# A block's forward and backward pass: issuing every TensorE product and transpose as four 32-column matmuls

## The chip, the cores and the metric

The kernel runs on one core of a Trainium2 chip. The time is the device time in microseconds (us) from the first to the last instruction of one execution. In the text PE is TensorE (PEld its weight loads), DVE is VectorE, ACT is ScalarE, POOL is GpSimd and SP is SyncE, as the profile names them.

## The reference

One transformer block with 2048 tokens of 512 features, in bfloat16: layer norm, local attention with 32 heads of 16 features over 8 earlier positions at a distance of 2, a residual, a second layer norm, a feed-forward part of width 1792 with GELU, and a second residual. The kernel returns the block's output and the gradients of the input and of six parameters.

```python
def _A_ref(x, wqkv, wo):                 # S=2048, H=32 heads, Dh=16, W=8, dil=2
    q, k, v = split_heads(x @ wqkv)
    idx = pos[:, None] - arange(W) * dil # -1e9 where idx < 0
    logits = einsum("bhsd,bhswd->bhsw", q, k[idx]) * Dh ** -0.5
    o = einsum("bhsw,bhswd->bhsd", softmax(logits), v[idx])
    return merge_heads(o) @ wo
def _B_ref(x, w1, b1, w2, b2):
    return gelu(x @ w1 + b1) @ w2 + b2
h = x + _A_ref(layernorm(x), A_wqkv, A_wo)
h2 = h + _B_ref(layernorm(h), B_w1, B_b1, B_w2, B_b2)
# outputs: h2 and the vjp of grad_out for A_x, A_wqkv, A_wo, B_w1, B_b1, B_w2, B_b2
```

## The kernel before

The 2048 tokens are worked on in four chunks of 512 (`CH`), a chunk as four tiles of 128 tokens. The code describes about 1970 operations (`op(...)`: an engine, an estimated time, a function that emits the instructions, and the buffers it reads and writes). The table `ORDER` at the end of the file is the order in which they are emitted, over all stages and engines at once, and `HOMES` gives each buffer its place in SBUF or its PSUM bank. `Plan.emit` goes through `ORDER`; each engine gets its own instructions in that order, and waits between engines follow from the buffers.

The stages overlap. Roughly, in the order of time:

- The first 156 us: per chunk the layer norm, the projections to q, k and v (`p1_proj`, L626, and `p1_v`), the transposes that bring tiles from token-major to feature-major form and back (`to_fm_tiles`, L416; `to_tm_store`, L434), the attention scores (`p1_attn`: VectorE multiplies, L479, and TensorE adds up with a 0/1 matrix, L487), the softmax sums (L702), the weighted sum of v (`p1_o`, whose `band` multiplies on VectorE, L518, and adds up on TensorE, L527), its transposes (`turn`, L543), the output projection and the second layer norm.
- 156 to about 325 us: the feed-forward part and its backward pass (`p2_h`, `p2_out`, `p2_bwd`), which are 512-column products on TensorE and elementwise work on VectorE and ScalarE.
- After that: the backward pass of the attention (`p3_go`, `p3_dots`, with row sums at L919; `p3_bands`, three more rounds of `band` and `turn` for the gradients of q, v and k; `p3_gl1`), and between its steps the weight gradients (`wg_group`), which depend on little and fill TensorE. The products of the last weight gradient (evicted to `wgsq`) end the program.

Names in the rows: `ps` is any PSUM bank; `prf`, `prb`, `prbo`, `prbq`, `prbv` and `prbk` are VectorE's products; `S` the 0/1 matrices; `kt`, `qt`, `ln`, `ost`, `gqs`, `gks`, `gvs` tiles that are transposed; `e` and `pp` the operands of the 128-column sums (L702 and L919); `gw1in`, `gw2in`, `xw1in`, `xw2in`, `ro`, `gq3in` reloaded operands of the weight gradients; `got` the gradient of the attention's output; `wz` a zeroed tile for fillers at the start, which are run while the first loads come in (`warm`, L311 and L316).

TensorE's matmul takes a stationary operand (a weight load, `LDWEIGHTS`) of up to 128 columns, each of which becomes an output partition, and streams the other operand, up to 512 columns, past it. Two forms stand in the kernel. In the full form, one load of 128 columns and one matmul write 128 partitions. In the quarter form, four loads of 32 columns and four matmuls, each into its own 32 partitions, do the same product; the profile shows them as `128*32`. Three kinds of work have the quarter form by need, since each quarter has its own operand or output (`cls=1`): the projections at L626 and the sums at L487 and L527. For the products that go through `mmul` with 512 columns (`cls=4`) `Plan.emit` chooses: a run of them between two operations of `cls=1` gets the quarter form (`quad`, L268), any other run the full form (L270). Products with 256 columns, transposes, the sums at L702 and L919 and the fillers always have the full form. In this order the two forms meet at 34 places of TensorE.

```python
                if o.cls == 4:
                    run.append(i)
                else:
                    if prev == 1 and o.cls == 1:
                        quad.update(run)
                    run, prev = [], o.cls
```

Of the kernel before, what the change touches and what calls it, by code (L numbers as in the profile page):

```python
# [10 lines left out]
P = 128  # L11
# [7 lines left out]
W = 8  # L19
# [42 lines left out]
class Plan:  # L62
# [7 lines left out]
    def sb(self, name, shape, dt=BF16):  # L70
        n = int(np.prod(shape[1:])) * (4 if dt == F32 else 2)
        b = Buf(name, "sb", shape, dt, (n + 63) // 64 * 64)
        self.bufs.append(b)
        return b
# [43 lines left out]
    def emit(self, order, homes):  # L118

        nc = self.nc  # L120
        assert sorted(order) == list(range(len(self.ops))) and len(homes) == len(self.bufs)
        at = {i: n for n, i in enumerate(order)}
        assert all(at[p] < at[o.i] for o in self.ops for p in o.preds)
        last = {}
        for i in order:
            for b in self.ops[i].bufs:
                if b.space != "fix":
                    last[id(b)] = at[i]
        ps = nc.alloc_psum_tensor("ps", [P, NBANK * BANK], F32).ap()
        for b, h in zip(self.bufs, homes):  # L130
            b.home = h if b.space == "ps" else self.base + h * 64
            assert b.home + b.need <= (NBANK if b.space == "ps" else self.top)
        quad, run, prev = set(), [], 0
        for i in order:
            o = self.ops[i]
            if o.eng == "PE":
                if o.cls == 4:
                    run.append(i)
                else:
                    if prev == 1 and o.cls == 1:  # L140
                        quad.update(run)
                    run, prev = [], o.cls
        live = []
        for n, i in enumerate(order):
            o = self.ops[i]
            for b in o.bufs:
                if b._ap is None and b.space != "fix":
                    live = [x for x in live if last[id(x)] >= n]
                    assert all(x.space != b.space or x.home + x.need <= b.home or b.home + b.need <= x.home for x in live), (b.name, o.tag)
                    live.append(b)  # L150
                    if b.space == "ps":
                        b._ap = ps[:, b.home * BANK:(b.home + b.need) * BANK]
                    else:
                        b._ap = nc.alloc_sbuf_tensor_at(f"{b.name}_{n}_{len(live)}", list(b.shape), b.dt, offset=b.home).ap()
            self.quad = i in quad
            o.fn()


# [1 line left out]
def kernel(  # L160
# [21 lines left out]
    V, A, T, G, SY = nc.vector, nc.scalar, nc.tensor, nc.gpsimd, nc.sync  # L182
# [20 lines left out]
    def cst(name, shape, dt=BF16):  # L203
        return nc.alloc_sbuf_tensor(name, list(shape), dt).ap()

    ident, Pmat, nident = (cst(n, [P, P]) for n in ("ident", "Pmat", "nident"))
# [36 lines left out]
    pl = Plan(nc, base, top)  # L243
# [19 lines left out]

    def mmul(out, l, r, start, stop):

        if pl.quad:
            for a in range(4):
                T.matmul(out[32 * a:32 * a + 32, :], lhsT=l[:, 32 * a:32 * a + 32], rhs=r, start=start, stop=stop, skip_group_check=True)  # L268
        else:
            T.matmul(out, lhsT=l, rhs=r, start=start, stop=stop, skip_group_check=True)  # L270

    def act_us(n, ptr=0, accum=False):
        return 0.055 + 0.833e-3 * n + 0.093 * ptr + (0.10 if accum else 0.0)
# [29 lines left out]
    def warm(n, more=0, each=2):  # L303

        z = sb("wz", [P, 512])
        pz = ps_("pwz")
        op("DVE", 0.2, lambda: V.memset(z(), 0.0), w=[z], tag="wz")

        def mm():
            for _ in range(n):  # L310
                T.matmul(pz(), lhsT=z()[:, 0:P], rhs=z(), start=True, stop=True)  # L311
        op("PE", 0.2157 * n, mm, r=[z], w=[pz], tag="warm")

        def mm2():
            for _ in range(each):
                T.matmul(pz(), lhsT=z()[:, 0:P], rhs=z(), start=True, stop=True)  # L316
        for _ in range(more):
            op("PE", 0.2157 * each, mm2, r=[z], w=[pz], tag="fill")

# [76 lines left out]
    def to_fm(src, dst, tag, soft=()):  # L396
        for hh in range(2):
            pt = ps_("pt" + tag)

            def tr(hh=hh, pt=pt):  # L400
                for d2 in range(2):
                    dc = 2 * hh + d2
                    for j in range(TPC):
                        T.transpose(pt.bf()[:, d2 * 512 + j * P:d2 * 512 + (j + 1) * P], src()[:, j, dc * P:(dc + 1) * P], ident[:])
            op("PE", 8 * XP, tr, r=[src, IDENT], w=[pt], tag="xp" + tag, soft=soft, lat=0.17)
            evict(dst, lambda hh=hh: dst()[:, 2 * hh:2 * hh + 2, :], pt, lambda pt=pt: pt.bf().rearrange("p (a n) -> p a n", a=2), 1024,
                  key=hh, tag="fm" + tag)

    def to_fm_tiles(src, dst, tag):

        for j in range(TPC):
            pt = ps_("pt" + tag)

            def tr(pt=pt, j=j):
                for dc in range(DC):
                    T.transpose(pt.bf()[:, dc * P:(dc + 1) * P], src()[:, j, dc * P:(dc + 1) * P], ident[:])  # L416
            op("PE", DC * XP, tr, r=[(src, j), IDENT], w=[pt], tag="xp" + tag, lat=0.17)
            evict(dst, lambda j=j: dst()[:, :, j * P:(j + 1) * P], pt, lambda pt=pt: pt.bf()[:, 0:512].rearrange("p (a n) -> p a n", a=DC), 512,
                  key=j, tag="fm" + tag)
# [5 lines left out]
    def to_tm_store(fm, off, dst, c, back, tag, pm):  # L425
        for j2 in range(TPC // 2):
            pt = ps_("ptm" + tag)

            def tr(j2=j2, pt=pt):
                for jj in range(2):  # L430
                    j = 2 * j2 + jj
                    for g in range(4):
                        o = _sub(pt.bf(), [[32, DH], [1, 8]], jj * 512 + 8 * g) if pm else pt.bf()[:, jj * 512 + g * P:jj * 512 + (g + 1) * P]
                        T.transpose(o, fm()[:, g, off + j * P:off + (j + 1) * P], (Pmat if pm else ident)[:])  # L434
            st = sb("tm" + tag, [P, 2, 512])
            op("PE", 8 * XP, tr, r=[(fm, 0), (fm, 1), PMAT if pm else IDENT], w=[pt], tag="xptm" + tag)
            evict(st, lambda st=st: st(), pt, lambda pt=pt: pt.bf().rearrange("p (a n) -> p a n", a=2), 1024, tag="tm" + tag)
            tm_store(st, dst, c, j2, back, tag)
# [97 lines left out]
    def turn(src, dst, mp, tag):  # L536

        pt = ps_("ptu" + tag)

        def tr():  # L540
            for mm in range(2):
                for k in range(4):
                    T.transpose(pt.bf()[:, mm * 512 + k * P:mm * 512 + (k + 1) * P], src()[:, 2 * mp + mm, k * P:(k + 1) * P], ident[:])  # L543
        op("PE", 8 * XP, tr, r=[(src, 2 * mp), (src, 2 * mp + 1), IDENT], w=[pt], tag="xpu" + tag)
        evict(dst, lambda: dst()[:, 2 * mp:2 * mp + 2, :], pt, lambda: pt.bf().rearrange("p (a n) -> p a n", a=2), 1024, key=mp, tag="un" + tag)

# [134 lines left out]
    def p1_attn(c):  # L681
# [4 lines left out]
        if c == 0:  # L686
            op("DVE", 0.25, lambda: V.tensor_tensor(out=L3()[0:32, :, 0:16], in0=L3()[0:32, :, 0:16], in1=mk[:], op=ALU.add), r=[MKB], w=[L], tag="mask")
        mx, e, r = sb("mx", [P, P]), sb("e", [P, W, P]), sb("r", [P, P])
        d["e"] = e
        op("DVE", 1.13, lambda: V.tensor_reduce(out=mx(), in_=L().rearrange("p (w n) -> p n w", w=W), axis=mybir.AxisListType.X, op=ALU.max),  # L690
           r=[L], w=[mx], tag="max")
# [6 lines left out]
        pss = ps_("pss", 1)  # L698

        def esum():  # L700
            for w in range(W):
                T.matmul(pss()[:, 0:P], lhsT=ident[:], rhs=e()[:, w, :], start=(w == 0), stop=(w == W - 1))  # L702
        op("PE", W * XP, esum, r=[e, IDENT], w=[pss], tag="sume")

        def recip():
# [4 lines left out]
           r=[e, r], w=[(attn, c)], tag="attn", lock=1)  # L710
# [188 lines left out]
    def p3_dots(c):  # L899
# [10 lines left out]
        pp = sb("pp", [P, W, P])  # L910
# [4 lines left out]
        pr_, sr = ps_("psr", 1), sb("sr", [P, P])  # L915

        def rowsum():
            for w in range(W):
                T.matmul(pr_()[:, 0:P], lhsT=nident[:], rhs=pp()[:, w, :], start=(w == 0), stop=(w == W - 1))  # L919
        op("PE", W * XP, rowsum, r=[pp, NID], w=[pr_], tag="rowsum")  # L920
        evict(sr, lambda: sr(), pr_, lambda: pr_()[:, 0:P], P, tag="rowsum")

        def sub():
# [4 lines left out]
           r=[L, (attn, c)], w=[(glf, c)], tag="glf")  # L928
# [169 lines left out]
    def wturn(dst, dap, src, sap, kb, key, tag):  # L1098

        pt = ps_("ptw" + tag)  # L1100

        def tr():
            for k in range(8):
                T.transpose(pt.bf()[:, k * P:(k + 1) * P], sap(k), ident[:])
        op("PE", 8 * XP, tr, r=[src, IDENT], w=[pt], tag="xp" + tag)
        evict(dst, dap, pt, lambda: pt.bf().rearrange("p (a n) -> p a n", a=kb), 1024, key=key, tag="ev" + tag)

# [4 lines left out]
    for i in range(0 if W2PE else 4):  # L1112
        r = F // 4
# [12 lines left out]
    for c in range(NC):  # L1126
        pl.stage = 9 + c
        if c == 1:
            xload(woR, lambda: woR(), lambda: A_wo, 512, tag="woT", soft=[(h_[3], 0)])
            op("ACT", act_us(4 * D), lambda: A.copy(out=woT().rearrange("p a (d h) -> p a d h", h=H), in_=_sub(woR()[:, 0, 0:1], [[D, DC], [1, DH], [DH, H]])),  # L1130
               r=[woR], w=[woT], tag="hinwo")
# [204 lines left out]
```

## Time and profile before

| | |
|---|---|
| median of three runs | 551.95 us (551.7 to 554.23) |
| span of the profiled execution | 551.9 us |
| TensorE busy | 538.8 us, 98%, 7764 matmuls |
| VectorE busy | 494.2 us, 90% |
| ScalarE busy | 324.2 us, 59% |
| mean granted TensorE clock | 0.997 |
| DMA moved | 126.68 MB, 230 GB/s |

The profile shows one execution; the only time of its own that it has is the span, from the first to the last instruction. Matmuls are pipelined: the profile shows each quarter or full matmul of 512 columns with 379 ns, though one begins every 216 ns where they follow each other. So the length of a chain piece, which goes from start to start, gives the price of a unit, and the mean duration doesn't.

### The profile page before, as it was taken

The page shows a single profiled execution, that of the slowest core. Times are in us where ns is not written, and L with a number is a line of the kernel's source. Part 1 is how long each engine was busy: PE and PEld are TensorE (multiplying, and loading weights), DVE is VectorE, ACT ScalarE, POOL GpSimd, SP SyncE. Part 2 cuts the span into 40 slices and gives each one's busy share as a digit, 9 for nine tenths or more (in the row PEclk, how much of TensorE's full clock was granted, in tenths as well). Part 3 has the DMA queues.
Part 4 walks back from the last instruction along what each step waited for, and adds up shares of the span by engine and source line. Part 5 has one row for each costly group of instructions (what it writes and reads, how often), then busy time and mean ns, then how long its engine had stood idle before and what let it go on. Part 6 is the DMA issues. An engine that isn't in the chain of part 4 may idle for free.

```text
span 551.9 us, 17462 instructions
## 1 busy us (share of the span) xinstructions
PE 538.8 (98%) x7764; PEld 286.7 (52%) x7764; DVE 494.2 (90%) x648; ACT 324.2 (59%) x507; POOL 25.8 (5%) x40
## 2 busy tenths in 40 slices
PE   7999999999989999999999999999999999999996
PEld 4756554444535445555555555465455555555542
DVE  7999999999979999999787089958899999999993
ACT  4987799989899876885341242034033376443521
POOL 1300100030001000000000000000010001000000
PEclk9999999999989999999999999999999999999999
DMA  8899998991597558679999999999999997888427
GB/s 279 226 291 281 417 302 190 201 332 83 74 235 251 137 98 197 201 121 214 197 191 219 182 194 192 291 218 281 213 279 425 335 338 284 355 290 187 128 60 190
DMA packets 195147, 126.68 MB, mean 230 GB/s; under 512 B 149760, under 2 KB 190656, under 8 KB 193024
## 3 DMA queue, kind: packets, MB, share of 16 engines
q1 hardware_dynamic: 189472, 81.79, 66.3%
q0 software_dynamic: 3408, 41.68, 19.8%
q10 hardware_dynamic: 2192, 2.10, 1.1%
q8 instruction: 60, 0.98, 0.8%
q14 instruction: 15, 0.12, 0.1%
HBM read 55.74 MB, written 35.21 MB: 165 GB/s over the span
## 4 chain that ended last, share of the span: by engine, by line
PE 55%; DVE 16%; ACT 4%; DMA 3%; issue 3%; SPq 2%; POOL 0%; ACTq 0%; DVEq 0%
PE ps L268 32%; PE ps L270 16%; PE ps L527 4%; DMA oT<-ost 2%; DVE xb L856 2%; DVE prbk L518 1%; DVE prbo L518 1%; DVE xb L803 1%; PE ps L487 1%; DVE prbv L518 1%; PE ps L543 1%; DVE x L799 1%; DVE st L360 1%; DVE h L747 1%; DVE h2s L828 1%
## 5 line engine op out<-in xcount | busy, mean ns | idle before, releaser
L479 DVE TENSOR_TENSOR prb<-got,vw 128x4096 bf16<-128x4096 bf16 x16 | 36.0, 2282 | 20.7 <-ACT got L297 13.8
L268 PE MATMUL ps<-w1T,xb 128*32 128x512 bf16 x896 | 53.1, 379 | 0.6 <-DVE h2s L828 0.4
L268 PE MATMUL ps<-goT,w2T 128*32 128x512 bf16 x832 | 50.5, 379 | 0.2 <-ACT xb L774 0.2
L297 ACT CAST wgs<-ps 128x512 bf16<-128x512 f32 (+1 forms) x30 | 16.2, 562 | 53.8 <-PE ps L270 30.4
L268 PE MATMUL ps<-w,gl 128*32 128x512 bf16 x776 | 46.3, 379 | 0.0
L856 DVE SCALAR_TENSOR_TENSOR xb<-xb,ps 128x512 bf16<-128x512 bf16 x56 | 36.9, 681 | 6.6 <-PE ps L268 6.4
L774 ACT ACTIVATE xb<-ps,b1c 128x512 bf16<-128x512 f32 x56 | 35.6, 703 | 10.1 <-PE ps L268 5.0
L268 PEld LDWEIGHTS <-xb 128*32 128x32 bf16 x896 | 26.2, 97 | 23.1 <-issue 1.2
L518 DVE TENSOR_TENSOR prbv<-Rv,cfv 128x4096 bf16<-128x4096 bf16 x16 | 35.7, 2284 | 1.4 <-PE ps L527 1.4
L518 DVE TENSOR_TENSOR prbq<-Rq,cfq 128x4096 bf16<-128x4096 bf16 x16 | 35.9, 2287 | 0.9 <-PE ps L270 0.4
L518 DVE TENSOR_TENSOR prbk<-Rk,cfk 128x4096 bf16<-128x4096 bf16 x16 | 35.9, 2284 | 0.3 <-PE ps L527 0.2
L518 DVE TENSOR_TENSOR prbo<-Ro,cfo 128x4096 bf16<-128x4096 bf16 x16 | 35.9, 2283 | 0.2
L479 DVE TENSOR_TENSOR prf<-qt,kt 128x4096 bf16<-128x4096 bf16 x16 | 35.7, 2283 | 0.0
L268 PEld LDWEIGHTS <-w2T 128*32 128x32 bf16 x832 | 24.0, 97 | 21.3 <-issue 0.5
L268 PEld LDWEIGHTS <-gl 128*32 128x32 bf16 x776 | 21.3, 97 | 21.1 <-ACT gl L777 1.3
L268 PE MATMUL ps<-wqkvT,gqkvT 128*32 128x512 bf16 x512 | 31.0, 379 | 0.0
L796 ACT ACTIVATE xb<-xb 128x2048 bf16<-128x2048 bf16 (+1 forms) x16 | 26.6, 1691 | 6.4 <-DVE xb L795 6.4
L626 PE MATMUL ps<-ln1T,wqk 128*32 128x512 bf16 x512 | 29.3, 381 | 0.7 <-ACT ln1T L297 0.7
L270 PE MATMUL ps<-ln2T,w 128*128 128x512 bf16 x120 | 27.4, 379 | 0.0
L792 ACT ACTIVATE x<-xb 128x2048 bf16<-128x2048 bf16 (+1 forms) x16 | 26.4, 1691 | 1.4 <-DVE h L747 1.3
L777 ACT ACTIVATE gl<-xb 128x2048 bf16<-128x2048 bf16 (+1 forms) x16 | 26.5, 1686 | 0.1
L561 ACT ACTIVATE gyr<-ps,rstd 128x512 bf16<-128x512 f32 x16 | 10.8, 677 | 23.5 <-PE ps L268 23.5
(199 smaller groups left out, 1085.7 us busy)
## 6 DMA issues: line engine op xcount, KB each, us to landing
Ro<-v_d POOLq DMA_DIRECT2D x4, 2304.0 KB, 11.6
Rq<-k_d POOLq DMA_DIRECT2D x4, 2304.0 KB, 11.5
Rv<-go_d POOLq DMA_DIRECT2D x4, 2304.0 KB, 13.9
Rk<-q_d POOLq DMA_DIRECT2D x4, 2304.0 KB, 14.1
g_d<-gl SPq DMA_DIRECT2D x9, 512.0 KB, 5.2
gh_d<-xb SPq DMA_DIRECT2D x9, 512.0 KB, 4.7
w<-in_B_w_dram SPq DMA_DIRECT2D x2, 1792.0 KB, 7.4
out_dram<-wgs SPq DMA_DIRECT2D x13, 256.0 KB, 4.7
```

The lines of the kernel that those rows point to most:

```text
L268: T.matmul(out[32 * a:32 * a + 32, :], lhsT=l[:, 32 * a:32 * a + 32], rhs=r, start=start, stop=stop, skip_group_check=True)
L270: T.matmul(out, lhsT=l, rhs=r, start=start, stop=stop, skip_group_check=True)
L297: fn = lambda: A.copy(out=ap(), in_=pap())
L479: op("DVE", tt_us(4096), lambda g=g, pr=pr: V.tensor_tensor(out=pr(), in0=ql()[:, g, :].unsqueeze(1).to_broadcast([P, W, 512]), in1=_sub(k ...
L518: V.tensor_tensor(out=pr().rearrange("p a j (d h) -> p a j d h", h=H), in0=_sub(R()[:, o0, 0:1], [[st, 2], [512, 4], [32, DH], [1, H]]), i ...
L527: T.matmul(ps()[32 * j:32 * j + 32, :], lhsT=S4[:], rhs=pr()[:, hf, j, :], start=(hf == 0), stop=(hf == 1), skip_group_check=True)
L626: T.matmul(ps()[32 * a:32 * a + 32, gg * 512:(gg + 1) * 512], lhsT=_sub(wq_()[:, dc, 0:1], [[DH, H]], sel * D + 4 * g + a), rhs=rhs, start ...
L774: op("ACT", act_us(512, 1), lambda f=f, ps=ps, xb=xb, f0=f0: A.activation(out=xb()[:, f - f0, :], in_=ps(), func=ACT.Identity, bias=b1c[:, ...
L777: op("ACT", act_us(N), lambda xb=xb, gl=gl: A.activation(out=fl(gl), in_=fl(xb), func=ACT.Gelu_apprx_tanh), r=[xb], w=[gl], tag="gelu", mo ...
L792: op("ACT", act_us(N), lambda xb=xb, x2=x2: A.activation(out=fl(x2), in_=fl(xb), func=ACT.Square), r=[xb], w=[x2], tag="x2")
L796: op("ACT", act_us(N), lambda xb=xb: A.activation(out=fl(xb), in_=fl(xb), func=ACT.Tanh, scale=GC), w=[xb], tag="tanh", mode=6)
L856: op("DVE", 0.61, lambda f=f, ps=ps, z=z, f0=f0: V.scalar_tensor_tensor(out=z()[:, f - f0, :], in0=z()[:, f - f0, :], scalar=1.0, in1=ps() ...
```

## The change

Every product that goes through `mmul`, the fillers, the sums at L702 and L919 and all transposes of 128 x 128 blocks (the new `turn128`) are issued in the quarter form. The choice in `Plan.emit` goes. `ORDER` and `HOMES` stay as they were, and no operation of another engine changes. The sums over eight blocks of 128 columns, formerly plain matmuls, go through `mmul` now. Two small transposes (of `b1b`, 14 rows, and `gbb`, 18 columns) keep their form. TensorE's matmuls after the change are 9224 of 512 columns, 256 of 256 and 1600 of 128, all in the quarter form, and the two small ones; before they were 6656 quarter ones of 512 columns, and 642 full ones of 512, 64 of 256 and 400 of 128.

```diff
-        quad, run, prev = set(), [], 0
-        for i in order:
...
-            self.quad = i in quad
             o.fn()
...
     def mmul(out, l, r, start, stop):
 
-        if pl.quad:
-            for a in range(4):
-                T.matmul(out[32 * a:32 * a + 32, :], lhsT=l[:, 32 * a:32 * a + 32], rhs=r, start=start, stop=stop, skip_group_check=True)
-        else:
-            T.matmul(out, lhsT=l, rhs=r, start=start, stop=stop, skip_group_check=True)
+        for a in range(4):
+            T.matmul(out[32 * a:32 * a + 32, :], lhsT=l[:, 32 * a:32 * a + 32], rhs=r, start=start, stop=stop, skip_group_check=True)
+
+    def turn128(out, src):
+
+        for a in range(4):
+            T.transpose(out[32 * a:32 * a + 32, :], src[:, 32 * a:32 * a + 32], ident[:])
...
-                T.matmul(pz(), lhsT=z()[:, 0:P], rhs=z(), start=True, stop=True)
+                mmul(pz(), z()[:, 0:P], z(), start=True, stop=True)
...
-                T.transpose(pt.bf()[:, dc * P:(dc + 1) * P], src()[:, j, dc * P:(dc + 1) * P], ident[:])
+                turn128(pt.bf()[:, dc * P:(dc + 1) * P], src()[:, j, dc * P:(dc + 1) * P])
...
-                    T.transpose(pt.bf()[:, mm * 512 + k * P:mm * 512 + (k + 1) * P], src()[:, 2 * mp + mm, k * P:(k + 1) * P], ident[:])
+                    turn128(pt.bf()[:, mm * 512 + k * P:mm * 512 + (k + 1) * P], src()[:, 2 * mp + mm, k * P:(k + 1) * P])
...
-                T.matmul(pss()[:, 0:P], lhsT=ident[:], rhs=e()[:, w, :], start=(w == 0), stop=(w == W - 1))
+                mmul(pss()[:, 0:P], ident[:], e()[:, w, :], start=(w == 0), stop=(w == W - 1))
...
-                T.matmul(pr_()[:, 0:P], lhsT=nident[:], rhs=pp()[:, w, :], start=(w == 0), stop=(w == W - 1))
+                mmul(pr_()[:, 0:P], nident[:], pp()[:, w, :], start=(w == 0), stop=(w == W - 1))
```

TensorE's instructions in the backward bands, at 446 us of the profiled execution, where the last sums of a band of v (`prbv`) are followed by eight transposes of the gradient of k (`gks`). Numbers behind a name only tell buffers apart. Before:

```order
L527 LDWEIGHTS S
L527 MATMUL ps<-prbv_36_7832,S 32x512
L543 LDWEIGHTS gks_38_7869
L543 MATMUL ps<-ident,gks_38_7869 128x128
L543 LDWEIGHTS gks_38_7869
L543 MATMUL ps<-ident,gks_38_7869 128x128
```

And the same place after the change, where line 261 is in `turn128`:

```order
L521 LDWEIGHTS S
L521 MATMUL ps<-prbv_36_10454,S 32x512
L261 LDWEIGHTS gks_38_10491
L261 MATMUL ps<-ident,gks_38_10491 32x128
L261 LDWEIGHTS gks_38_10491
L261 MATMUL ps<-ident,gks_38_10491 32x128
L261 LDWEIGHTS gks_38_10491
L261 MATMUL ps<-ident,gks_38_10491 32x128
L261 LDWEIGHTS gks_38_10491
L261 MATMUL ps<-ident,gks_38_10491 32x128
```

Nothing has moved: the two full transposes of the first piece are eight quarter ones now, the first four of which stand in the second piece, and the change of form between the sums and the transposes is gone.

TensorE's instructions in the first chunk's projections, where the last transposes of the normed input (`ln`, L416) are followed by the projection to k (`wqk`), before and then after:

```order
L416 LDWEIGHTS ln_0_23_7_136
L416 MATMUL ps<-ident,ln_0_23_7_136 128x128
L626 LDWEIGHTS wqk_6_134
L626 MATMUL ps<-ln1T_36_11_159,wqk_6_134 32x512
L626 LDWEIGHTS wqk_6_134
```

```order
L261 MATMUL ps<-ident,ln_0_23_7_166 32x128
L261 LDWEIGHTS ln_0_23_7_166
L261 MATMUL ps<-ident,ln_0_23_7_166 32x128
L620 LDWEIGHTS wqk_6_164
L620 MATMUL ps<-ln1T_36_11_213,wqk_6_164 32x512
```

The projection itself is as it was; what stands ahead of it has four times as many instructions.

More of the change, by code (lines that the diff above doesn't have):

```diff
@@ L132, in emit @@
             assert b.home + b.need <= (NBANK if b.space == "ps" else self.top)
-        quad, run, prev = set(), [], 0
-        for i in order:
[L135 to L138, printed above, removed]
-                else:
-                    if prev == 1 and o.cls == 1:
-                        quad.update(run)
-                    run, prev = [], o.cls
         live = []
@@ L264, in mmul @@
     def mmul(out, l, r, start, stop):
-        if pl.quad:
-            for a in range(4):
-                T.matmul(out[32 * a:32 * a + 32, :], lhsT=l[:, 32 * a:32 * a + 32], rhs=r, start=start, stop=stop, skip_group_check=True)
-        else:
-            T.matmul(out, lhsT=l, rhs=r, start=start, stop=stop, skip_group_check=True)
+        for a in range(4):
[3 more added lines that the diff above has]
+            T.transpose(out[32 * a:32 * a + 32, :], src[:, 32 * a:32 * a + 32], ident[:])
     def act_us(n, ptr=0, accum=False):
@@ L315, in mm2 @@
             for _ in range(each):
-                T.matmul(pz(), lhsT=z()[:, 0:P], rhs=z(), start=True, stop=True)
+                mmul(pz(), z()[:, 0:P], z(), start=True, stop=True)
         for _ in range(more):
@@ L403, in tr @@
                     for j in range(TPC):
-                        T.transpose(pt.bf()[:, d2 * 512 + j * P:d2 * 512 + (j + 1) * P], src()[:, j, dc * P:(dc + 1) * P], ident[:])
+                        turn128(pt.bf()[:, d2 * 512 + j * P:d2 * 512 + (j + 1) * P], src()[:, j, dc * P:(dc + 1) * P])
             op("PE", 8 * XP, tr, r=[src, IDENT], w=[pt], tag="xp" + tag, soft=soft, lat=0.17)
@@ L433, in tr @@
                         o = _sub(pt.bf(), [[32, DH], [1, 8]], jj * 512 + 8 * g) if pm else pt.bf()[:, jj * 512 + g * P:jj * 512 + (g + 1) * P]
-                        T.transpose(o, fm()[:, g, off + j * P:off + (j + 1) * P], (Pmat if pm else ident)[:])
+                        if pm:
+                            T.transpose(o, fm()[:, g, off + j * P:off + (j + 1) * P], Pmat[:])
+                        else:
+                            turn128(o, fm()[:, g, off + j * P:off + (j + 1) * P])
             st = sb("tm" + tag, [P, 2, 512])
@@ L1103, in tr @@
             for k in range(8):
-                T.transpose(pt.bf()[:, k * P:(k + 1) * P], sap(k), ident[:])
+                turn128(pt.bf()[:, k * P:(k + 1) * P], sap(k))
         op("PE", 8 * XP, tr, r=[src, IDENT], w=[pt], tag="xp" + tag)
```

## The prediction

> **What bounds the kernel now.** I read the page's busy times and its chain first, then the busy times by stage, then the idle times of VectorE (DVE) and the chain piece by piece in the second half. In the fence below, the first row is busy time, share of the span and instructions of each engine, the second the chain's shares, the rest busy time by stage (window, PE, PEld, DVE, ACT, POOL, granted clock, DMA share, GB/s).
>
> ```profile
> PE 538.8 (98%) x7764; PEld 286.7 (52%) x7764; DVE 494.2 (90%) x648; ACT 324.2 (59%) x507; POOL 25.8 (5%) x40
> PE 55%; DVE 16%; ACT 4%; DMA 3%; issue 3%; SPq 2%; POOL 0%; ACTq 0%; DVEq 0%
> ...
> 0.00:156.00 156.00, 148.38 (x1763) 82.75 (x1767) 150.18 (x189) 133.81 (x181) 15.23 (x22) 1.00 0.85 241
> 156.00:283.00 127.00, 126.41 (x2296) 65.31 (x2297) 117.69 (x235) 91.56 (x115) 1.48 (x1) 0.99 0.83 184
> 283.00:394.00 111.00, 110.76 (x1578) 59.85 (x1578) 80.39 (x95) 30.49 (x71) 1.13 (x2) 1.00 1.10 220
> 394.00:500.00 106.00, 105.95 (x1598) 55.17 (x1594) 103.51 (x64) 49.76 (x95) 6.88 (x13) 1.00 0.93 322
> 500.00:541.00 41.00, 41.00 (x520) 20.92 (x520) 40.06 (x64) 15.86 (x42) 0.00 (x0) 1.00 0.51 119
> ```
>
> TensorE (PE) is busy almost everywhere, at full clock, so it looks like the only bound. But VectorE is as full in two stages: 150.2 of the first 156 us, 103.5 of the 106 us from 394 to 500. There both set the time, and a shorter TensorE only waits for VectorE. TensorE alone binds from 283 to 394 us (VectorE 80.4 of 111) and after 500 us, where its last products need little of VectorE.
>
> VectorE's idle pieces after 394 us, with what ended them in brackets:
>
> ```profile
> 394.26 1.13 DVE L497 STREAM_TRANSPOSE cfq<-glf 128x512 bf16<-128x512 bf16 x1 [2.25 <-DMA tmgod<-got]
> ...
> 420.99 6.70 DVE L518 TENSOR_TENSOR prbq<-Rq,cfq 128x4096 bf16<-128x4096 bf16 x3 [0.36 <-PE ps L270]
> 435.36 2.29 DVE L518 TENSOR_TENSOR prbv<-Rv,cfv 128x4096 bf16<-128x4096 bf16 x1 [1.08 <-PE ps L527]
> ...
> 506.24 2.29 DVE L518 TENSOR_TENSOR prbv<-Rv,cfv 128x4096 bf16<-128x4096 bf16 x1 [0.28 <-PE ps L527]
> ```
>
> From 436 to 506 us VectorE never waits for TensorE: a gain of TensorE there can't move it.
>
> **What a unit of TensorE costs.** Call one former 128-column matmul, or four 32-column ones that take its place, a unit. The chain (start, us, what) gives its price in both forms, and that of a change of form:
>
> ```profile
> 283.25 38.60 PE ps L268 x712
> ...
> 339.12 1.83 PE ps L270 x8
> ...
> 417.86 0.45 PE ps L543 x8
> 418.30 3.45 PE ps L270 x16
> ...
> 426.55 0.55 PE ps L527 x8
> ...
> 431.43 3.45 PE ps L268 x64
> ...
> 523.91 17.39 PE ps L270 x80
> ```
>
> Sixteen full products of 512 columns take 3.45 us, 216 ns each; 64 quarter ones take 3.45 us too, 216 ns for four. So in the 512-column products (624 of L270 in 18 groups, of which the first and the last stand here, and 18 fillers) the two forms cost the same: 0 for these, with a long sustained case behind it (712 in 38.60 us, 54 ns per quarter). Eight full transposes take 0.45 us, 56 ns each.
>
> ```profile
> L270 PE MATMUL ps<-ln2T,w 128*128 128x512 bf16 x120 | 27.4, 379 | 0.0
> ...
> L270 PE MATMUL ps<-gqs,ln1b 128*128 128x512 bf16 x4 | 1.0, 382 | 0.0
> ```
>
> A change of form shows as a surcharge: 1.83 instead of 1.73 us for eight full products after quarter ones, 0.55 instead of 0.43 for eight quarter ones after transposes. It is 0.10 to 0.12 us, and the chain shows it where the neighbours follow without a wait.
>
> **The change, part by part.**
>
> (1) Changes of form that go. TensorE's order has 34 places where a full unit and a quarter unit meet: 19 before 156 us, four between 339 and 381 us, ten between 409 and 476 us, one at 523.91 us. At about 0.1 us each that is 3.4 us of TensorE's time. What reaches the end:
> - The 19 before 156 us: VectorE is at 150.2 of 156 us there; TensorE's gain turns into idle time before VectorE's next product. I take 0.
> - The four at 339 to 381 us: 0.4 us of TensorE, while VectorE waits for it. But VectorE's next stop, at 394.26 us, is a transfer of got (2.25 us), which was made earlier. Between 0 and 0.4; I take 0.1, since that transfer is what ends the wait.
> - The ten at 409 to 476 us: 1.0 us of TensorE. Two of them lie before the wait of 1.08 us at 435.36 us and shorten it by 0.2; the other eight fall where VectorE doesn't wait. I take 0.2.
> - The one at 523.91 us: 0.12 (17.39 against 80 x 0.216 = 17.28), all of it at the end, since only wgq products and their eviction follow.
> - The wait at 506.24 us, 0.28 us for a product buffer that TensorE frees, may go in part: 0.1.
> Sum: -0.5 us, between -0.1 and -3.4.
>
> (2) The transposes and the sums of 128 columns. These rows (count, busy, mean ns) are the units whose price in the new form the trace doesn't show:
>
> ```profile
> L416 PE MATMUL ps<-ident,ln 128*128 128x128 bf16 x64 | 5.7, 219 | 1.3 <-DVE ln L385 0.5 <-ACT kt L297 0.3 <-DVE r L707 0.3
> L434 PE MATMUL ps<-ident,qt 128*128 128x128 bf16 x64 | 4.9, 219 | 0.0
> L434 PE MATMUL ps<-ident,kt 128*128 128x128 bf16 x64 | 4.7, 219 | 0.0
> L543 PE MATMUL ps<-ident,gqs 128*128 128x128 bf16 x48 | 3.5, 219 | 0.0
> L702 PE MATMUL ps<-e,ident 128*128 128x128 bf16 x32 | 2.5, 219 | 0.0
> L543 PE MATMUL ps<-ident,gks 128*128 128x128 bf16 x32 | 2.5, 219 | 0.0
> L543 PE MATMUL ps<-ident,gvs 128*128 128x128 bf16 x32 | 2.4, 219 | 0.0
> L919 PE MATMUL ps<-pp,nident 128*128 128x128 bf16 x32 | 2.4, 219 | 0.0
> L543 PE MATMUL ps<-ident,ost 128*128 128x128 bf16 x32 | 2.3, 219 | 0.0
> L270 PE MATMUL ps<-gw1in,ln 128*128 128x256 bf16 x48 | 6.4, 273 | 0.0
> L270 PE MATMUL ps<-xw1in,ln 128*128 128x256 bf16 x16 | 2.2, 273 | 0.0
> ```
>
> That is 400 units of 128 columns: 64 + 128 + 32 + 32 = 256 before 156 us (ln, kt, qt, e, ost), 112 + 32 = 144 after 339 us (gqs, gks, gvs, pp), and 64 of 256 columns between 363 and 381 us. Each becomes four loads and four matmuls where there were one and one: 8 instructions in 56 ns, 7 ns each, if the price stays. The fastest steady stream in the trace is the quarter products' 216 / 8 = 27 ns per instruction. So the price lies between 56 ns (the four column groups run side by side and only the array's columns count) and 216 ns (the steady issue of 27 ns is a limit). Below 56 nothing speaks: the columns streamed are the same. The trace also shows bursts; after a wait, seven loads of the quarter form start so close that all are over in 0.12 us:
>
> ```profile
> 499.97 0.12 PEld L527 LDWEIGHTS <-S 128*32 128x32 bf16 x7 [0.34 <-issue]
> ...
> L527 PEld LDWEIGHTS <-S 128*32 128x32 bf16 x512 | 13.6, 96 | 14.2 <-issue 2.0 <-DVE prbk L518 0.4 <-DVE prbq L518 0.4
> ```
>
> One load lasts 96 ns, so the seven starts lie within some 25 ns, with matmuls between them: under 4 ns per instruction, when they stand ready. It also says that the loads of four column groups run together. Since the runs of 128-column units are short (8 here, 64 instructions after the change) and lie between 512-column units, I take 56 ns, nearer to the burst: cost 0. Of the end at 216 ns, 400 x 160 ns = 64 us and 64 x (216 - 109) ns = 6.8 us, more below.
>
> The Trainium skill, "TensorEngine Tiling (Array Packing)", section "Restrictions", says that column tiling switches the fast weight load off. By it and by the load time in the Trainium skill, "TensorE: Matmul & The Clock Gate", section "LDWEIGHTS (loading the stationary operand)" (columns / 1.2 ns), four loads of 32 columns one after another would be an estimated 107 ns, and 400 units would cost 20 us more. The burst above disagrees with "one after another".
>
> (3) The fillers (18 units of 512 columns at the start) and the wider instruction stream. TensorE's instructions go from 15530 to 22166 rows, VectorE's 567 and ScalarE's 396 stay. The extra 6636 have to be fetched; the fetches lie beside other transfers, so 0. Evictions still wait for a unit's last matmul: 0. Two small transposes (b1b, gbb) keep their form.
>
> **Sum.** 551.9 (span of the profiled execution) - 0.5 + 0 = 551.4 us. The median of the three runs, 551.95, is the same as the span, so nothing is to be added around it. No change that a measurement of this kernel tells from noise (about 0.5%, 2.8 us).
>
> **Rivals.**
>
> The one wait of TensorE at the start, which no rival can use up:
>
> ```profile
> PE ps L311 <- DVE wz L307: 2.0, 1, 2.0
> ```
>
> A. The issue of instructions limits the short units (slower). Place: every run of 128-column units; price: if a load and a matmul together need 27 ns, half of the sustained 54, a unit costs 108 instead of 56 ns, and the 256-column units (109 ns) are just not touched. It decides from about 14 ns per instruction on. Before 156 us: 256 x 52 = 13.3 us, less TensorE's idle 7.6 - 2 (start) and 1.9 of changes of form, +5.8 us; after: 144 x 52 = 7.5 less 1.6 = +5.9 us. Together 563.6 us; what stands ready ahead of a run hides up to all of it, so 553 to 564, say 560. For it: nothing in the trace issues faster than 27 ns for long. Against it: the bursts.
> The Trainium skill, "TensorE: Matmul & The Clock Gate", section "Wait — 56ns, not 53.3ns?", states a floor of about 25 ns from matmul to matmul however short they are, which would make a unit 100 ns and agrees with this rival; the trace's starts within a group of four lie closer than that, so for matmuls in different column groups it doesn't hold as written.
>
> B. The same with the sustained 27 ns per instruction as the limit (much slower): 216 ns for each short unit. Before 156 us 256 x 160 = 41 us less 7.5 = +33; after 144 x 160 + 64 x 107 = 29.9 us less 1.6 = +28. That is about 613 us. For it: the quarter stream runs at just this rate. Against it: that stream is exactly as fast as the full one, 216 ns, which has two instructions a unit, so the array explains it.
>
> C. All changes of form are worth their price (faster): 551.9 - 3.4 = 548.5 us. It needs VectorE to start earlier in the first 156 us and from 436 to 506 us, where it is full; TensorE's waits speak for it only at 506 us.
>
> **Chances.** My forecast (550.3 to 552.9 us) 0.60; A 0.21, of which 0.03 within 0.5% of before; B 0.11; C 0.08, all counted as faster. So faster 0.08, same 0.63, slower 0.29. The range from 549.5 to 565 holds the forecast and all of A (0.81) and leaves out B and C.
>
> **What would show it.** Right: in the changed kernel eight former transposes (now 32 matmuls) take 0.45 us in the chain, 216 ns stay for all 512-column units, no surcharge of 0.1 us is left, and TensorE's busy time falls by 2 to 3 us while its idle time before products of VectorE (L527's and L487's successors) grows by nearly as much. Wrong: the transposes' 32 matmuls take 0.8 us or more (A) or 1.7 us (B); ScalarE's evictions and VectorE would then wait for TensorE in the first 156 us, and VectorE's busy share there would fall below 150 of 156 us. The forecast fails most easily in the price of a short unit, the one number that no row of before shows.

## The result, and the profile after

The changed kernel takes 571.25 us (566.62 to 596.3, five runs), against 552.13 us (551.7 to 554.23, five runs) for the kernel before on the same chip: a ratio of 1.031, with a 95% interval of 1.029 to 1.034. It is slower by 17 us by the ratio (19 by the medians), where 551.4 us and no measurable change were forecast. A second job gave 575.88 us against 552.47 (ratio 1.037, 1.029 to 1.044), 20 us by the ratio. Times here are medians of all executions, while the ratios leave out disturbed ones, such as the one of 596.3 us that was profiled first. The profile shown is that of the second job; its execution has a time of 574.08 us and a span of 572.3 us.

The page's busy times, and then the busy time by stage (window, PE, PEld, DVE, ACT, POOL, granted clock, DMA share, GB/s):

```profile
PE 541.1 (95%) x11082; PEld 314.3 (55%) x11082; DVE 495.0 (86%) x648; ACT 325.1 (57%) x507; POOL 25.8 (5%) x40
```

```profile
0.00:156.00 156.00, 139.97 (x3174) 89.45 (x3178) 137.24 (x173) 122.08 (x163) 14.63 (x21) 0.98 0.82 232
156.00:283.00 127.00, 124.82 (x2301) 62.44 (x2297) 121.67 (x222) 95.88 (x119) 2.07 (x2) 1.00 0.82 180
283.00:394.00 111.00, 110.77 (x2249) 68.19 (x2245) 80.68 (x118) 35.30 (x77) 1.13 (x2) 1.00 1.11 208
394.00:500.00 106.00, 97.71 (x2121) 56.51 (x2117) 92.36 (x60) 45.62 (x88) 5.83 (x11) 1.00 0.95 312
500.00:572.30 72.30, 67.83 (x1256) 37.73 (x1248) 63.02 (x78) 26.24 (x64) 2.16 (x4) 0.98 0.65 166
```

VectorE has the same work (495.0 us against 494.2) and loses its place in two stages: 137.2 of the first 156 us where it had 150.2, and 92.4 of the 106 us after 394 where it had 103.5. That is 24 us, a little more than the span has grown (20.4 us). Between 283 and 394 us TensorE is as busy as it was (110.8 of 111 us).

What TensorE itself waited for (line and releaser, us in total, times, longest):

```profile
PE ps L261 <- issue: 8.4, 5, 3.1
PE ps L256 <- issue: 7.0, 5, 1.7
PE ps L256 <- DVE wz L298: 2.0, 1, 2.0
PE ps L521 <- issue: 1.7, 2, 1.3
...
PE ps L620 <- issue: 0.6, 1, 0.6
```

In 13 places TensorE stood still for "issue", that is, for nothing that the profile shows as a wait: 17.7 us together. The list of before has no such row; its longest are the 2.0 us for `wz` and 2.0 us for a transfer. Some of the places after the change, in TensorE's timeline (start, us, what, and in brackets the idle time before it):

```profile
71.65 0.59 PE L261 MATMUL ps<-ident,qt 128*32 128x128 bf16 x24
75.31 0.29 PE L261 MATMUL ps<-ident,qt 128*32 128x128 bf16 x2 [3.07 <-issue]
...
84.52 0.51 PE L261 MATMUL ps<-ident,kt 128*32 128x128 bf16 x22
87.80 0.34 PE L261 MATMUL ps<-ident,kt 128*32 128x128 bf16 x10 [2.76 <-issue]
...
101.16 2.55 PE L256 MATMUL ps<-ln2T,w 128*32 128x512 bf16 x44
105.36 2.12 PE L256 MATMUL ps<-ln2T,w 128*32 128x512 bf16 x36 [1.66 <-issue]
```

TensorE stops in the middle of a run: 22 and 10 of the 32 matmuls of one operation's transposes stand on either side of a gap, 44 and 36 matmuls of a run of products with `w` on either side of another. The profile names no operand that was waited for. The price of the units, in the chain:

```profile
431.63 0.45 PE ps L261 x32
432.07 3.45 PE ps L256 x64
435.53 0.45 PE ps L261 x32
...
544.51 20.75 PE ps L256 x384
```

Thirty-two quarter matmuls, which are eight former transposes, take 0.45 us: 56 ns a unit. The 512-column units take 216 ns (20.75 us for 96). No surcharge of a change of form is left between them. So the units cost what the forecast said, and the time is lost between instructions for which the profile shows no wait.

The queues of transfers name the difference. Before, and then after (packets, MB, share of the 16 engines):

```profile
q8 instruction: 60, 0.98, 0.8%
```

```profile
q8 instruction: 86, 1.41, 1.1%
```

Each packet of this queue carries 16 KB, and 26 more packets for 6636 more instructions are one for every 255. So it fetches TensorE's instructions in blocks of about 256. Taking every packet's end from the trace and laying it beside TensorE's starts, I find for all 13 gaps of this execution that TensorE resumes 1.26 to 1.56 us after a packet has ended, and that it always stops at the same place of a block: after 447 matmuls and loads, and a whole number of 256 more, in front, and after 429 and a whole number of 256 at the back. (The 18 between are presumably the few other instructions of TensorE, which the count leaves out.) For the gap before 75.31 us the packet lies at 72.78 to 73.74 us; the queues of the window from 72.6 to 73.9 us show it:

```profile
q8 instruction: 1, 0.02, 4.6%
```

That is 4.6% of 16 engines for 1.3 us, or 0.96 us. The theory, called F in the expectations: where TensorE's instructions come densely, it uses up a block before the next is there, and stands still for the rest.

### The profile page after: what moved, and what is told of

Same layout as the page of the kernel before. It is cut to its first block, busy times and chain, and to the rows that moved or that the text cites. A ratio compares the mean times of both kernels' runs of the same rounds, so it can differ in the third digit from the quotient of the medians.

```text
span 594.5 us, 24098 instructions
## 1 busy us (share of the span) xinstructions
PE 545.4 (92%) x11082; PEld 315.4 (53%) x11082; DVE 495.3 (83%) x648; ACT 324.9 (55%) x507; POOL 25.8 (4%) x40
## 3 DMA queue, kind: packets, MB, share of 16 engines
q0 software_dynamic: 3408, 41.68, 20.4%
## 5 line engine op out<-in xcount | busy, mean ns | idle before, releaser
L256 PE MATMUL ps<-gw1in,ln 128*32 128x512 bf16 (+1 forms) x768 | 44.2, 368 | 18.9 <-DMA gw1in<-gh_d 14.1
L256 PE MATMUL ps<-ln2T,w 128*32 128x512 bf16 x896 | 53.6, 385 | 1.5 <-issue 1.5
L256 PE MATMUL ps<-goT,w2T 128*32 128x512 bf16 x896 | 54.7, 379 | 0.0
L256 PE MATMUL ps<-w,gl 128*32 128x512 bf16 x896 | 53.2, 379 | 1.0 <-ACT gl L771 0.9
L256 PEld LDWEIGHTS <-ln 128*32 128x32 bf16 x1024 | 31.0, 100 | 41.0 <-issue 24.6
L256 PE MATMUL ps<-wqkvT,gqkvT 128*32 128x512 bf16 x768 | 48.1, 379 | 0.0
L768 ACT ACTIVATE xb<-ps,b1c 128x512 bf16<-128x512 f32 x56 | 35.7, 697 | 12.3 <-PE ps L256 9.5
L256 PE MATMUL ps<-gor,gw2in 128*32 128x512 bf16 x672 | 38.9, 379 | 0.0
L256 PEld LDWEIGHTS <-w 128*32 128x32 bf16 x896 | 25.6, 98 | 25.1 <-issue 3.9
L256 PEld LDWEIGHTS <-gl 128*32 128x32 bf16 x896 | 24.7, 97 | 25.2 <-ACT gl L771 3.2
L256 PEld LDWEIGHTS <-ln1b 128*32 128x32 bf16 x768 | 23.4, 97 | 20.5 <-issue 2.5
## 6 DMA issues: line engine op xcount, KB each, us to landing
Rq<-k_d POOLq DMA_DIRECT2D x4, 2304.0 KB, 10.3
```

Of the source, the lines that this page charges most:

```text
L768: op("ACT", act_us(512, 1), lambda f=f, ps=ps, xb=xb, f0=f0: A.activation(out=xb()[:, f - f0, :], in_=ps(), func=ACT.Identity, bias=b1c[:, ...
```

## The experiments

F was set against two others: that the number of instructions or of quarter matmuls itself costs (N), and that the short units are slow to issue (rival A of the prediction, called P in the expectations). All ratios are to the kernel before on the same chip.

**The changed kernel again**, for a profile and a second time.

> The changed kernel once more, for a profile of an execution at the usual time. Theory F (fetch): TensorE's instructions are fetched in blocks of 256 (16 KB); where a block holds many 128-column units it is used up in 2 to 4 us, before the next block has landed, and TensorE stands still with nothing to wait for but the fetch. It expects 566 to 572 us, 128-column units still at 56 ns, and about ten standstills of 1 to 5 us, each ending 1.3 to 1.5 us after a fetch of 16 KB has ended. Theory P (price): the quarter form of a 128-column unit takes 108 ns or more throughout; it expects few standstills and 400 units of twice the length (+20 us).

Measured: 575.88 us, 1.037 (1.029 to 1.044), above the range of F; the profile is the one above. Its 13 standstills of 0.4 to 3.1 us, each ending soon after a packet, are those that F expects, and its units of 56 ns are not the 108 that P needs.

**Only the wide units in quarter form.** The 400 units of 128 columns go back to the full form.

```diff
     def turn128(out, src):
-        for a in range(4):
-            T.transpose(out[32 * a:32 * a + 32, :], src[:, 32 * a:32 * a + 32], ident[:])
+        T.transpose(out, src, ident[:])
...
-                mmul(pss()[:, 0:P], ident[:], e()[:, w, :], start=(w == 0), stop=(w == W - 1))
+                T.matmul(pss()[:, 0:P], lhsT=ident[:], rhs=e()[:, w, :], start=(w == 0), stop=(w == W - 1))
```

> All products of 512 and 256 columns and the fillers in the quarter form, the 400 units of 128 columns (transposes and the sums at L702 and L919) back in the full form. Instructions of TensorE: 19.8 thousand against 15.5 and 22.2; changes of form: 72 against 36 (before) and 4. F: no block lasts under about 5 us, so no standstill; the changes of form cost TensorE 3.6 us more than before, some of it hidden: 552 to 556 us. Theory N (number): the loss grows with the number of instructions, whatever they are; 4236 of the 6636 extra ones give 64% of 19 us: 564 us.

Measured: 556.95 us, 1.006 (1.004 to 1.008). The median lies just above F's 552 to 556, the ratio gives a loss of 3.3 us, inside it. The run has 77 fetches of instructions, 17 more than before, yet one standstill of 0.2 us is left:

```profile
PE ps L256 <- issue: 0.2, 1, 0.2
```

The loss comes with 72 places where the form changes, 38 more than before. In its trace a full transpose behind a quarter product starts 312 ns after it, where 216 pass without a change, and a quarter product behind a full transpose 149 ns after it, where 56 pass: 0.09 to 0.10 us each, some 3.6 us for 38. So the 64% of the extra instructions that it has cost little or nothing as long as they come at 27 ns each. N, which expects 564 us, falls.

**Only the short units in quarter form.** The choice of `Plan.emit` is kept for `mmul`; the transposes and the sums over blocks of 128 columns get a quarter form of their own.

```diff
     def mmul(out, l, r, start, stop):
+        if pl.quad:
+            for a in range(4):
+                T.matmul(out[32 * a:32 * a + 32, :], lhsT=l[:, 32 * a:32 * a + 32], rhs=r, start=start, stop=stop, skip_group_check=True)
+        else:
+            T.matmul(out, lhsT=l, rhs=r, start=start, stop=stop, skip_group_check=True)
+
+    def mshort(out, l, r, start, stop):
         for a in range(4):
```

> Only the 400 units of 128 columns in the quarter form; products full or quarter as before the change. Instructions: 17.9 thousand; changes of form: 78. F: most of the loss, 558 to 568 us, with standstills at the runs of transposes, fewer than in the changed kernel since full products between them spread the instructions out. N: 36% of 19 us, 559 us, spread evenly. P: the whole loss or more.

Measured: 562.75 us, 1.017 (1.013 to 1.020). Standstills inside the short units:

```profile
PE ps L280 <- issue: 3.6, 3, 2.4
...
PE ps L275 <- issue: 2.3, 1, 2.3
```

They are 5.9 us in four places, with only 70 fetches, seven fewer than in the kernel with the wide units. (Twelve more of 0.16 us each, at L270, are places where the trace has lost the record of a full matmul; it has 608 of 642.) The loss is 9.2 us by the ratio, 10.3 by the medians, inside F's range. The rest of it, 3 to 4 us, is about what the changes of form cost: the trace has 76, 42 more than before.

**Dense instructions without any short unit.** In the kernel before, the 192 products of the weight gradient of q, k and v (`wg_group`, tag `q`) all take the quarter form, which 116 of them had already, and each quarter's weights are loaded three times more than needed. What is computed stays the same, but 20 instructions stand in 216 ns, 10.8 ns each. Two weaker doses load them once more than needed (12 instructions, 18 ns each) and just once (8, 27 ns).

```diff
-                    mmul(ps()[:, 0:N], l, r, start=(n == 0), stop=(n == k - 1))
+                    if tag == "q":
+                        for a in range(4):
+                            for _ in range(3):
+                                T.ldweights(l[:, 32 * a:32 * a + 32], tile_position=(0, 32 * a))
+                            T.matmul(ps()[32 * a:32 * a + 32, 0:N], lhsT=l[:, 32 * a:32 * a + 32], rhs=r, start=(n == 0), stop=(n == k - 1),
+                                     skip_group_check=True)
+                    else:
+                        mmul(ps()[:, 0:N], l, r, start=(n == 0), stop=(n == k - 1))
```

> The kernel before, with the 192 product units of the last three weight gradients (wgq, 512 columns) in the quarter form and each of their quarter loads issued four times instead of once: the same products, no 128-column unit changed, 20 instructions in 216 ns there, 10.8 ns each, so that 80 units in a row at the end use up six blocks of 256 in 2.8 us each. The extra loads have no use. F: standstills of 1 to 4 us about every 256 instructions after 523 us, 560 to 575 us in all. P and N-free theories (the 128-column units themselves are slow, or instructions cost nothing while the array is busy): 551 to 554 us.

> The control for e3: the same 192 products in the quarter form, each quarter load once, 8 instructions in 216 ns, 27 ns each. Changes of form 45 against 36. F: a block lasts 6.9 us, no standstill, 551 to 554 us. If the quarter form of these products were itself the cause in e3: as e3, 565 us.

> e3 with each quarter load twice: 12 instructions in 216 ns, 18 ns each, a block in 4.6 us. F: between e4 and e3; the changed kernel's fetches began 0.5 to 7 us after TensorE had used up what makes room for them and took 2.4 us more until their instructions ran, so only the late ones are felt: one to three standstills of 0.5 to 2 us, 552 to 557 us.

Measured:

| instructions | time, us | ratio (95%) | fetches | `issue` in these products |
|---|---|---|---|---|
| 27 ns each | 552.56 | 1.001 (0.999 to 1.003) | 62 | none |
| 18 ns each | 553.96 | 1.0025 (1.001 to 1.004) | 65 | 0.2 us, once |
| 10.8 ns each | 564.76 | 1.020 (1.015 to 1.024) | 71 | 8.8 us, six times |

The densest kernel's waits and its last products:

```profile
PE ps L1003 <- issue: 8.8, 6, 2.7
```

```profile
547.57 1.46 PE L1003 MATMUL ps<-gks,ln1b 128*32 128x512 bf16 x21
550.10 3.01 PE L1003 MATMUL ps<-gks,ln1b 128*32 128x512 bf16 x51 [1.08 <-issue]
555.20 4.08 PE L1003 MATMUL ps<-gks,ln1b 128*32 128x512 bf16 x40 [2.08 <-issue]
```

This is the run that settles it. No unit is short that was not short before, no transpose has changed, the products keep their 216 ns but for one stretch at half clock behind the last gap; only the instructions come closer together, and TensorE stands still in runs of 512-column products, once more 1.3 to 1.6 us after a packet's end in all six places. Rival A has nothing to say here. That the weaker doses pass almost free shows that neither the quarter form of these products nor a second load is what costs. All three times lie in F's ranges. Of the densest kernel's loss, 10.8 us by the ratio and 12.3 by the medians, 8.8 are standstills; the stretch at half clock (3.41 us, worth 1.7) and nine more changes of form (0.9) make up most of the rest.

**Half of the short units each.** From the changed kernel, either the 256 short units before 156 us get the full form again, or the 144 after 339 us.

```diff
+    def full128(out, src):
+
+        T.transpose(out, src, ident[:])
...
-                    turn128(pt.bf()[:, dc * P:(dc + 1) * P], src()[:, j, dc * P:(dc + 1) * P])
+                    full128(pt.bf()[:, dc * P:(dc + 1) * P], src()[:, j, dc * P:(dc + 1) * P])
```

> The changed kernel with the 256 units of 128 columns of the first 156 us (transposes of ln, kt, qt and ost, sums at L702) back in the full form; the 144 of the second half stay in the quarter form. F: the standstills of the first 156 us go, those after 430 us stay (three of 1.7 to 2.1 us in the profile of e0): 556 to 560 us. If the number of instructions decided: 20.6 of 15.5 to 22.2 thousand, 77% of the loss, 566 us.

> The reverse: the 256 units of the first 156 us in the quarter form, the 144 of the second half full. F: five standstills of 1.4 to 3.3 us before 110 us and the half clock behind the longer ones stay, those after 430 us go: 563 to 568 us. If the number of instructions decided: 21.3 thousand, 87% of the loss, 568 us. The two losses together should be about that of the changed kernel plus the changes of form that come back (e1: 3 us for all).

Measured, quarter form kept at the back: 562.2 us, 1.018 (1.012 to 1.024), above F's range; kept in front: 565.62 us, 1.023 (1.017 to 1.029), inside it. The first has four standstills, all after 394 us, the second eight, of which seven lie before 156 us. Busy time by stage, back first, then front:

```profile
0.00:156.00 156.00, 150.18 (x2617) 84.92 (x2617) 149.33 (x187) 132.83 (x180) 15.23 (x22) 1.00 0.88 242
394.00:500.00 106.00, 98.44 (x2124) 55.65 (x2119) 96.15 (x60) 48.05 (x92) 6.88 (x13) 0.98 0.87 303
```

```profile
0.00:156.00 156.00, 141.90 (x3237) 92.95 (x3241) 140.68 (x177) 124.76 (x168) 14.63 (x21) 0.99 0.80 232
394.00:500.00 106.00, 105.24 (x1896) 56.85 (x1888) 99.11 (x64) 47.47 (x92) 6.35 (x12) 1.00 0.98 319
```

In each, TensorE loses time in the stage that has the dense runs; in the other stage it is about as busy as before, though VectorE has 4 us less in the second kernel's back stage (the window is fixed, and its work comes later). By the ratios the two losses are 9.9 and 12.7 us, together 22.6, as expected somewhat more than the changed kernel's 17 to 20, which has no changes of form at these units. The times alone do not decide here: the first lies between F's range and N's 566 us, and the second is as near to N's 568. What speaks for F is where the standstills are. The first came out above F's range because its standstills (6.4 us) come with other things: a stretch of 3.41 us at half clock from 479.7 us, eight changes of form more than before, and a new wait of 1.2 us for `prbv`. Their parts were not separated.

**Is a shorter TensorE worth anything?** Part (1) of the prediction said hardly: 0 before 156 us, 0.2 at the back. Two kernels leave out computation to ask: one accumulation step of four in the projection to q (16 units, 3.46 us, before 156 us), or half of the v part of the input gradient in the first two chunks (16 units, 3.46 us, between 438 and 480 us).

```diff
-                    for dc in range(DC):
+                    nd = DC - (sel == 0)
+                    for dc in range(nd):
...
```

```diff
-                    for b in range(4):
+                    for b in range(2 if i == 1 and c < 2 else 4):
```

> The kernel before with one of the four accumulation steps of each projection to q left out (16 units at L626 between 10 and 73 us, 3.46 us of TensorE; q lacks a quarter of its input). It asks what TensorE's time before 156 us is worth. My prediction's reading (VectorE sets the time there): at most 0.7 us gained, 551 to 552.5 us. Rival (TensorE sets it): 2.5 to 3.5 us gained, 549 us.

> The kernel before with half of the v part of the input gradient left out in the first two chunks (16 units of wqkvT and gqkvT between 438 and 480 us, 3.46 us of TensorE). It asks the same of the stretch from 436 to 506 us. My reading (VectorE is full there and waits for nothing of TensorE's): at most 0.7 us gained. Rival: 2.5 to 3.5 us gained, 549 us.

Measured: 552.59 us, 1.0002 (0.9986 to 1.0019), and 551.49 us, 0.998 (0.996 to 1.0003). By the medians 0 and 0.8 us of 3.46 come back, against at most 0.7 expected; the intervals allow up to 0.8 and 2.3 us, so the second is less sure. In the first, TensorE's busy time before 156 us falls while VectorE's stays:

```profile
0.00:156.00 156.00, 144.74 (x1683) 82.95 (x1695) 149.78 (x189) 133.01 (x181) 15.23 (x22) 1.00 0.86 241
```

That is 3.6 us less for TensorE (148.38 before) and 0.4 for VectorE: the time taken away has become waiting.

## Why the prediction was wrong

- **Part (3) failed, "the extra 6636 have to be fetched; the fetches lie beside other transfers, so 0".** It asked whether the transfers had room, and they had (queue q8 takes 1.1%). It did not ask whether a block arrives in time. By the trace of the changed kernel a fetch begins, at the earliest, with some 305 instructions left to run; the packet takes about 1.0 us (0.9 to 2.4), TensorE goes on 1.3 to 1.6 us after it, and ahead of the standstills the packet itself begins 2.6 to 7.3 us later than that. At 27 ns the 305 instructions last 8.2 us, and no fetch of before is late: the shortest stretch of 256 takes 6.7 us there, packets begin at most about 5 us late, and the closest one lands about 3 us before its block is reached, where 1.3 to 1.6 are needed. At 18 ns they last 5.5 us, at 10.8 ns 3.3 us, and in a run of short units at 7 ns 2.1 us, less than packet and restart need even without a delay. What the step put at 0 measured 13 standstills, 17.7 us, in the profiled execution. The sign that the prediction had named for rival A, VectorE's share before 156 us falling below 150 us, came (137.2), but from these standstills and not from the units' price.
- The page "Runtime: NRT & Kernel Launch" of the Trainium skill, section "Instruction fetch mechanics", describes the refill in blocks of 256 and calls it mostly hidden. The blocks agree with the 255 instructions per packet; "hidden" holds here at 27 ns per instruction and fails at 10.8 and 7 ns.
- **Part (2), the price of a short unit, was right**: 56 ns, where 56 to 216 had been possible. Rivals A and B are false as mechanisms. A's range (553 to 564) comes nearer to the time than the forecast, because it names runs of short units, which use the blocks up (though only 5 of the 13 standstills end at a transpose), and instructions too close together; that is luck as far as its mechanism goes. But its limit per instruction does not exist: a run goes at 7 ns until its block is used up.
- **Part (1) held as far as it was tested.** The changes of form are gone, and two cuts of 3.46 us of TensorE's time gave 0 and 0.8 us; no run took away the changes of form alone. The reverse does not hold: the kernel with the wide units has 38 more of them and loses 3.3 us, nearly their whole price. A reading that fits, but was not followed to the places: where two engines are both full, time taken from one is not gained, and time given to it is lost, since the other cannot work ahead. "What would show it" had counted on TensorE's busy time to fall by 2 to 3 us; it went from 538.8 to 541.1, or to about 538 without the stretches at half clock (below), so this sign did not come. Why is open.
- **A small miss:** the time of an execution lies 1.7 to 3.3 us above its span, mostly 1.8 to 2.0 (574.08 and 572.3 in the profile above; 551.92 and 550.1 in the kernel with single loads), and the prediction had taken the two as equal. That is 2 us, within what was called no change.

The sum for the profiled execution of after: 17.7 us of standstills, and two stretches of 3.41 us at half clock, worth 1.6 and 1.7 us by TensorE's busy time in them, make 21.0 of the 22.1 us by which its span exceeds the median span of before in the same job (550.2 us). The sum takes each lost microsecond as fully on the path and counts no gain for the changes of form; what these leave out is not assigned.

## What to carry to other kernels

Count TensorE's instructions per microsecond, not only the array's columns: a block of 256 has to last longer than its fetch takes from request to restart. In this kernel 192 products at 27 ns per instruction cost nothing that could be measured, at 18 ns 0.25% and at 10.8 ns 2% of the whole time, and the change with its runs of short quarter units at 7 ns 3 to 4%. The quarter form costs no array time (216 ns for 512 columns and 56 for 128, as in the full form), but four times the instructions of a short unit are not free; keep the full form where units are short and stand in long runs, and look for `issue` gaps in the middle of a run with all operands ready.

## What the runs showed of the hardware

- A transpose of 128 columns as four quarter ones takes 56 ns with its eight instructions, as long as the full one with its two (0.45 us for eight units in both forms).
- After some of the long standstills TensorE goes on at half clock. The granted clock (third figure from the end of a row) in the 3.4 us after three of the gaps of the changed kernel:

```profile
75.30:78.70 3.40, 3.39 (x43) 1.94 (x45) 3.37 (x3) 1.93 (x2) 0.00 (x0) 0.54 1.08 335
87.80:91.20 3.40, 3.40 (x95) 2.23 (x99) 2.25 (x3) 2.57 (x4) 0.00 (x0) 0.63 0.02 5
105.40:108.80 3.40, 3.40 (x64) 1.87 (x67) 2.40 (x3) 2.96 (x3) 0.00 (x0) 1.00 1.03 259
```

After gaps of 3.07 and 2.76 us it is 0.54 and 0.63, after one of 1.66 us it is 1.00. The half clock itself lasts 3.41 us each time, from 75.01 us, just ahead of the end of its gap, and from 88.67, 0.9 us behind it. The gap need not be one of fetching: in the kernel before, a wait of 1.96 us for a transfer, up to 155.94 us, is followed by half clock from 156.32 to 159.74 us. The length alone does not decide: in the kernel with dense loads a gap of 2.08 us was followed by 0.56, and gaps of 2.68 and 2.40 us by 1.00. The Trainium skill, "TensorE: Matmul & The Clock Gate", section "What's actually happening", has the clock fall after an idle window of about 3.4 us that runs freely. A free-running window agrees with lengths that don't decide; that a gap of 2.08 us is enough shows that a window need not be idle throughout.
- Why a packet of instructions begins up to 7 us after its block could have been asked for was not tried. Other transfers keep the engines busy in these stretches (a DMA share of 0.9 to 1.1), but no run took them away; and from 283 to 394 us of the changed kernel the share is as high (1.11), yet packets begin only 0.5 to 3.7 us late, so the share alone does not set the delay.
